# A layer of spectral mixing and two expert layers on one core: y's blocks turned by VectorE and carried by the regrouping DMAs

## The chip, the cores and the metric

One core of a Trainium2 chip runs the whole program. The metric is the time of one execution in microseconds, as the median of several; the profile is of one more execution. TensorE (PE), VectorE (DVE), ScalarE (ACT) and GpSimd (POOL) compute; SyncE (SP) issues nearly all DMAs, in order, on one queue. Each engine runs its own instructions in order and waits for the others by semaphores.

## The reference

An array x of 8 x 3072 x 256 goes through three layers; the random inputs are float32.

```python
X = np.fft.rfft(x, axis=1)                    # 1: spectral mixing
Yr = Xr @ w_r - Xi @ w_i + b_r;  Yi = Xr @ w_i + Xi @ w_r + b_i
Y = shrink(Yr, 0.01) + 1j * shrink(Yi, 0.01)
y = np.fft.irfft(Y, n=3072, axis=1)           # 24576 tokens of 256
h = y @ w_in                                  # 2: 256 -> 2048
x = (h - np.tanh(h)) @ w_out                  #    2048 -> 256
logits = x @ phi                              # 3: 32 slots
d = softmax(logits, axis=0)                   # over the tokens
slot_in = d.T @ x                             # 32 x 256
slot_out = experts(slot_in)                   # 8 experts, relu
out = softmax(logits, axis=1) @ slot_out
```

The second layer's output is never stored. Since x = y M - g w_out, with g = tanh(h) and M = w_in w_out, the slots' inputs can be had from running sums of d.T @ g (2048 features) and of d.T @ y (256 features), over all tokens.

## The kernel before

The program has a spectral phase, a token phase and an expert phase. The change lies in the token phase, which runs from about 700 to 2130 us in the profiled execution. It goes through 48 chunks (nch) of 512 tokens. Of each chunk it computes the 2048 gates g from y (the matmuls of L771, by a seven-product scheme, evacuated by ScalarE at L782 and added to by VectorE at L789, then tanh at L793), the logits (L892 from g, L900 from the raw y, tile yr), their running softmax over tokens, and two updates: `accum` adds d.T @ g to acc, `accum_y` adds d.T @ y to accy.

For an update TensorE needs tokens on the partitions, but gates and y have features there. Gates are turned in two steps. VectorE turns 32x32 blocks (`turn_g`, L846) into a tile gt: four feature pairs (p = 0 to 3) make the first half, p = 4 to 7 the second, 8 blocks of 32 features each. Then `regroup` (L860) moves each half by 16 DMAs of SyncE, from 32 partitions to 32 partitions, into four tiles gq. gt is one pool tag with two buffers, used in turn by the halves. The update `dg_mm` (L1020, tile pd) reads gq and the exponentials et.

y is turned in another way: `turn_y` (step TY, two calls a chunk) has TensorE transpose four 128x128 blocks of yr (L812) into a bank pd, and ScalarE copies the bank into a tile yq (L813). `dy_mm` (step DY, L828) multiplies it into unused columns of the logits' bank, and stands right ahead of `dg_mm`.

The order of all this is written out by hand in the table PLAN (L29 to L42). `chunk(c)` walks it once a chunk; an entry such as ("TY", -1, 0) calls `turn_y` for chunk c - 1, and one that has been done is skipped. On each engine the instructions stand in the order of these calls. A buffer's next writer waits for its readers. In the row of a chunk SyncE issues, in order: the first half's regrouping of the running chunk ("reg", 0, 0), a small store, the load of the next y, the second half's regrouping of the chunk before ("reg", -1, 1), and the load of the raw y ("loadr", 0). The step ("D", -1) follows ("DY", -1), and both come some way behind ("reg", -1, 1).

The last chunk takes another way: its gates are turned by TensorE (`turn_pe`) and so is its y.

`turn_exp` keeps the running sum of exponentials, ssum, with one scalar_tensor_tensor a chunk (L972).

Of the kernel before, what the change touches and what calls it, by code (L numbers as in the profile page):

```python
# [26 lines left out]


PLAN = (  # L29
# [8 lines left out]
    ("reg", -1, 1), ("W", 0, 3), ("splitt", 1, 0), ("comb", -1), ("P", 0, 3, 7),  # L38
# [3 lines left out]
)  # L42
TOKENS_BESIDE = {-4: 1, -2: 1, 0: 1, 1: 2, 2: 3, 3: 4}
# [590 lines left out]
def token_phase(tc, nch, yd, wh, wl, wp, wy, ident, ew):  # L634
# [9 lines left out]
    with ExitStack() as ctx:  # L644
# [175 lines left out]
        def dy_mm(c):  # L820


            beside = c < nch - 1
            o = dy[c] = lp[c + 1][:, 256:320] if beside else bank()[:, 0:64]
            y = yq.pop(c)
            for k in range(4):
                for a in (3, 2, 1, 0):
                    nc.tensor.matmul(  # L828
                        o[32 * a:32 * a + 32], ex[c][:, k, :], y[:, a, k], start=k == 0 and not beside, stop=k == 3,
                        skip_group_check=True,  # L830
                    )

        def accum_y(c):
# [3 lines left out]
            else:  # L837
                nc.vector.tensor_copy(accy, o)

        def turn_g(c, p):  # L840
            g = gs[c, p]
            if (c, p // 4) not in gt:
                gt[c, p // 4] = gtp.tile([128, 16, 8, 32], F32, tag="gt", name="gt")
            t = gt[c, p // 4]
            for u in range(2):
                nc.vector.transpose(out=t[:, :, 2 * (p % 4) + u, :], in_=g[:, u, :].rearrange("p (c i) -> p c i", i=32))  # L846

# [4 lines left out]
        def regroup(c, h):  # L852

            t = gt.pop((c, h)).rearrange("p (k q) f i -> p q k (f i)", q=4)
            if h == 0:
                gq[c] = [ew.gq_tile([128, 4, 512]) for _ in range(4)]
            for a in range(4):
                o = gq[c][a][:, :, 256 * h:256 * h + 256]
                for q in range(4):
                    nc.sync.dma_start(out=o[32 * q:32 * q + 32], in_=t[32 * a:32 * a + 32, q])  # L860

        def turn_pe(c, p, engines):

            if p // 4 not in gl:
                gl[p // 4] = gtp.tile([128, 4, 4, 256], F32, tag="gt", name="gl")
            o = gl[p // 4].rearrange("p k a (f i) -> p k f a i", i=32)
            for u in range(2):
                t = bank()
                for k in range(4):
                    k = slice(128 * k, 128 * k + 128)  # L870
                    nc.tensor.transpose(t[:, k], gs[c, p][:, u, k], ident)
                src = t.rearrange("p (k a i) -> p k a i", k=4, a=4)
                dst = o[:, :, 2 * (p % 4) + u]
                if engines[u] is nc.scalar:
                    nc.scalar.activation(dst, src, AF.Copy)
                else:
                    engines[u].tensor_copy(dst, src)
# [86 lines left out]
        def turn_exp(c):  # L964
            e, rs, a = le[c][64:128], rss.pop(c), al.get(c)
            et = sp.tile([128, 4, 32], F32, tag="et", name="et", bufs=1)
            for r in range(2):
                nc.vector.transpose(
                    out=et[64 * r:64 * r + 64].rearrange("p k s -> p (k s)"), in_=e[:, 128 * r:128 * r + 128]
                )  # L970
            if c:
                nc.vector.scalar_tensor_tensor(  # L972
                    out=ssum[0:64], in0=ssum[0:64], scalar=a[0:64], in1=rs, op0=ALU.mult, op1=ALU.add
                )
                nc.vector.tensor_copy(a[64:128], a[0:64])
            else:
                nc.vector.tensor_copy(ssum[0:64], rs)
            ex[c] = et
# [31 lines left out]
        def dg_mm(c):  # L1010

            o = dp[c] = ps2.tile([128, 512], F32, tag="d", name="pd")
            if c < nch - 1:
                parts = [(slice(0, 512), gq.pop(c))]
            else:
                parts = [(slice(256 * h, 256 * h + 256), [gl[h][:, :, a] for a in range(4)]) for h in range(2)]
            for f, g in parts:
                for k in range(4):
                    for a in (3, 2, 1, 0):
                        nc.tensor.matmul(  # L1020
                            o[32 * a:32 * a + 32, f], ex[c][:, k, :], g[a][:, k], start=k == 0, stop=k == 3
                        )
            del ex[c]
# [20 lines left out]
        def do(name, k, *args):  # L1044
# [5 lines left out]
            "P": wino, "A": add, "G": gate, "T": turn_g, "L": logit_mm, "D": dg_mm, "acc": accum, "sum": sum_l,  # L1050
            "sum2": sum_l2, "max": soft_max, "exp": soft_exp, "turnexp": turn_exp, "comb": combine,
            "cexp": combine_exp, "cend": combine_end, "loady": load_y, "rawt": raw_t, "splity": split_y,
            "lowy": low_y, "splitt": split_t, "reg": regroup, "loadr": load_raw, "TY": turn_y, "DY": dy_mm,
            "accy": accum_y,
        }

        def chunk(c):

            for name, d, *args in PLAN:
                k = c + d  # L1060
                if name == "S":

                    if c == 1:
                        split_sw(*args)
                elif name == "W":
                    if c == nch - 1:
                        weights(*args)
                elif k > 0 and k < nch or k == 0 and name not in "PAG":
                    if k < nch - 1 or name not in ("T", "reg"):
                        if c < nch - 1 or name not in ("D", "DY", "accy"):  # L1070
                            do(name, k, *args)
                    if c == 1 and (name, k, *args) == ("L", 0, 4):
                        do("L", 0, 6)
# [121 lines left out]
class ExpertWeights:  # L1195
# [61 lines left out]

    def load_ct(self, c0, c1):
        n = c1 - c0
        u = self.gtp.tile([128, n, 128], F32, tag="gt", name="ect") if c0 else self.gq_tile([128, n, 128])  # L1260
        for c in range(c0, c1, 16):
            m = min(c + 16, c1)
            self.tc.nc.sync.dma_start(out=u[:, c - c0:m - c0], in_=self.ctd[:, c:m])
        for c in range(c0, c1, 8):
            self.cts[c] = u[:, c - c0:c - c0 + 8]
# [5 lines left out]
    def pieces(self, j, home):  # L1271
        def tile(pool, tag, n=1024, **kw):
            t = pool.tile([128, n], F32, tag=tag, name="ewt", **kw)
            return [t[:, 512 * i:512 * i + 512] for i in range(n // 512)]

        if home in self.spare:
            return self.spare.pop(home)
        if home == "t":
            return [u for n in ("th", "tl") for i in range(2) for u in tile(self.txp, f"{n}{i}", 512)]
        if home[0] == "w":  # L1280
            return [u for n in ("wh", "wl") for i in range(2) for u in tile(self.wp, f"{n}{i}{home[1]}", 512)]
        if home == "y":
            return [u for t in ("y", "yh") for u in tile(self.yp, t)]
        if home[0] == "s":
            return tile(self.tyq, home, 1536)
        if home == "gt":
            r = tile(self.gtp, "gt", 4096)
            self.spare["gt"] = r[4:]
            return r[:4]
        if home == "gq":  # L1290
            t = self.gq_tile([128, 2048])
            return [t[:, 512 * i:512 * i + 512] for i in range(4)]
        return [u for i in range(2) for u in tile(self.txp, f"x{(2 * j + i) % 4}")]
# [203 lines left out]
```

## Time and profile before

| | |
|---|---|
| time, median of 3 runs | 2262.81 us (2259.74 to 2264.0) |
| the profiled execution's own time | 2261.4 us |
| its span | 2259.6 us |
| TensorE busy | 2210.0 us (98%) |
| weight loads of TensorE | 1819.3 us (81%) |
| VectorE busy | 1764.8 us (78%) |
| ScalarE busy | 1456.5 us (64%) |
| GpSimd busy | 656.5 us (29%) |
| packets of SyncE's DMA queue | 77.6% of 16 engines' span |

The profile lists each instruction with its engine, line, tiles (out<-in, buffer numbers left out) and shape. The chain that ended last is followed back from the last instruction: it names at each step what released it. PE's and weight loads' busy times overlap. Matmuls are pipelined, so several in a row have starts closer together than one's duration: in a row of TensorE the start of the next row tells what a group took of the engine. [...]

### The profile page before, as it was taken

The page shows a single profiled execution, that of the slowest core. Times are in us where ns is not written, and L with a number is a line of the kernel's source. Part 1 is how long each engine was busy: PE and PEld are TensorE (multiplying, and loading weights), DVE is VectorE, ACT ScalarE, POOL GpSimd, SP SyncE. Part 2 cuts the span into 40 slices and gives each one's busy share as a digit, 9 for nine tenths or more (in the row PEclk, how much of TensorE's full clock was granted, in tenths as well). Part 3 has the DMA queues.
Part 4 walks back from the last instruction along what each step waited for, and adds up shares of the span by engine and source line. Part 5 has one row for each costly group of instructions (what it writes and reads, how often), then busy time and mean ns, then how long its engine had stood idle before and what let it go on. Part 6 is the DMA issues. An engine that isn't in the chain of part 4 may idle for free.

```text
span 2259.6 us, 51262 instructions
## 1 busy us (share of the span) xinstructions
PE 2210.0 (98%) x19832; PEld 1819.3 (81%) x19832; DVE 1764.8 (78%) x3557; ACT 1456.5 (64%) x2395; POOL 656.5 (29%) x666
## 2 busy tenths in 40 slices
PE   6999999999999999999999999999999999999989
PEld 3678888887888888888888888888888888888747
DVE  3999988988995787787777877877778778777634
ACT  2456666666556677777766777676767676767524
POOL 1334333443443322222222222222222222222111
PEclk8999999999999999999999999999999999999999
DMA  8778899898657777777777777778777777777899
GB/s 227 233 226 264 250 267 277 245 261 269 201 186 211 179 168 178 179 181 181 184 172 176 175 178 179 178 180 189 171 177 177 175 179 177 182 186 173 243 341 366
DMA packets 404019, 471.17 MB, mean 209 GB/s; under 512 B 36160, under 2 KB 351808, under 8 KB 403392
## 3 DMA queue, kind: packets, MB, share of 16 engines
q1 hardware_dynamic: 403664, 467.85, 77.6%
q8 instruction: 157, 2.57, 0.5%
q14 instruction: 86, 0.70, 0.1%
q10 hardware_dynamic: 112, 0.04, 0.0%
HBM read 164.45 MB, written 106.17 MB: 120 GB/s over the span
## 4 chain that ended last, share of the span: by engine, by line
PE 87%; DVE 5%; DMA 4%; issue 2%; SPq 1%; ACT 0%; POOL 0%; DVEq 0%; POOLq 0%; ACTq 0%
PE ph L771 41%; PE pl L892 8%; PE pd L1020 8%; PE pmix L322 5%; PE pi L407 4%; PE pf L248 4%; PE pf L281 3%; PE p_out L1319 3%; PE pi L379 3%; PE pa L322 2%; PE pd L812 2%; DMA ewt<-in_moe_w 1%; PE pl L828 1%; DVE sw L372 1%; PE pl L900 1%
## 5 line engine op out<-in xcount | busy, mean ns | idle before, releaser
L782 ACT ACTIVATE g<-ph 128x512 f32<-128x512 f32 x752 | 448.0, 596 | 379.5 <-PE ph L771 354.5
L789 DVE TENSOR_TENSOR g<-ph,g 128x512 f32<-128x512 f32 x564 | 373.3, 676 | 157.7 <-PE ph L771 147.2
L846 DVE STREAM_TRANSPOSE gt<-g 128x512 f32<-128x512 f32 x752 | 476.2, 681 | 13.0 <-DMA gq<-gt 6.5
L771 PE MATMUL ph<-th,s 128*128 128x256 f32 x2256 | 482.0, 286 | 2.1 <-ACT g L782 2.1
L771 PEld LDWEIGHTS ph<-th,s 128*128 128x128 f32 x2256 | 377.8, 189 | 41.4 <-issue 19.4
L793 ACT ACTIVATE g<-g 128x1024 f32<-128x1024 f32 x376 | 392.2, 1053 | 1.5
L771 PE MATMUL ph<-tl,s 128*128 128x256 f32 x1128 | 318.3, 282 | 0.0
L771 PE MATMUL ph<-y,wh 128*128 128x256 f32 x1128 | 316.4, 280 | 0.0
L771 PE MATMUL ph<-yh,wl 128*128 128x256 f32 x1128 | 315.7, 280 | 0.0
L771 PE MATMUL ph<-yh,wh 128*128 128x256 f32 x1128 | 315.7, 280 | 0.0
L684 POOL TENSOR_TENSOR tl<-tr,th 128x512 fp32r<-128x512 f32 x94 | 121.8, 1297 | 383.8 <-ACT th L683 350.3
L372 POOL TENSOR_TENSOR sw<-t,c 64x256 f32<-64x256 f32 x192 | 169.5, 883 | 170.1 <-DVE c L364 131.3
L771 PEld LDWEIGHTS ph<-tl,s 128*128 128x128 f32 x1128 | 213.9, 190 | 0.0
L771 PEld LDWEIGHTS ph<-yh,wh 128*128 128x128 f32 x1128 | 212.8, 189 | 0.1
L771 PEld LDWEIGHTS ph<-yh,wl 128*128 128x128 f32 x1128 | 212.4, 188 | 0.0
L771 PEld LDWEIGHTS ph<-y,wh 128*128 128x128 f32 x1128 | 212.3, 188 | 0.1
L678 POOL TENSOR_TENSOR tr<-y 128x256 f32<-128x256 f32 x92 | 67.8, 737 | 470.3 <-DMA y<-yd 470.3
L892 PE MATMUL pl<-g,wp 128*32 128x256 f32 x3072 | 195.4, 383 | 0.0
L1020 PE MATMUL pd<-gq,et 128*32 128x512 f32 x1504 | 183.8, 598 | 2.1 <-DMA gq<-gt 2.1
L669 POOL TENSOR_TENSOR y<-y,yh 128x1024 fp32r<-128x1024 f32 x46 | 110.6, 2403 | 182.9 <-issue 182.8
L407 PEld LDWEIGHTS pi<-i,v 96*128 96x128 f32 x1024 | 127.5, 191 | 26.0 <-issue 20.8
L281 PEld LDWEIGHTS pf<-f,a 128*128 128x128 f32 x768 | 102.5, 195 | 54.3 <-issue 40.9
(225 smaller groups left out, 4586.0 us busy)
## 6 DMA issues: line engine op xcount, KB each, us to landing
gq<-gt SPq DMA_DIRECT2D x1504, 128.0 KB, 2.5
xt<-in_x SPq DMA_DIRECT2D x64, 384.0 KB, 5.4
vd<-vs SPq DMA_DIRECT2D x96, 256.0 KB, 3.3
v<-vd SPq DMA_DIRECT2D x64, 384.0 KB, 5.4
yd<-yt SPq DMA_DIRECT2D x48, 512.0 KB, 5.6
y<-yd SPq DMA_DIRECT2D x48, 512.0 KB, 4.9
yr<-yd SPq DMA_DIRECT2D x48, 512.0 KB, 3.7
a<-ad SPq DMA_DIRECT2D x47, 512.0 KB, 6.0
```

Of the source, the lines that this page charges most:

```text
L281: nc.tensor.matmul(p[:, :, h, gg, :], t[:, gg, 128 * h:128 * h + 128], f2[:, 128 * g:128 * g + 128], start=True, stop=True,)
L322: nc.tensor.matmul(o, st[u], w[m], start=first and k == 0, stop=last and k == 2)
L372: eng.tensor_tensor(out=v[64 * ri:64 * ri + 64, gg], in0=t[q, e], in1=c[q, e], op=ALU.subtract)
L407: nc.tensor.matmul(p[:, a, :], t[:, 4 * u + a, :], i2[:, 96 * n2:96 * n2 + 128], start=True, stop=True)
L684: nc.gpsimd.tensor_tensor(out=lo, in0=t, in1=hi.bitcast(F32), op=ALU.subtract)
L771: nc.tensor.matmul(o[:, 256 * j:256 * j + 256], a[u][:, 128 * j:128 * j + 128], y[v], start=new and j == 0 and k == 0, stop=n in (2, 3, 4) ...
L782: nc.scalar.activation(e[n], o.rearrange("p (j n) -> p j n", j=2), AF.Copy)
L789: nc.vector.tensor_tensor(out=h, in0=o, in1=h, op=ALU.add)
L793: nc.scalar.activation(g, g, AF.Tanh)
L846: nc.vector.transpose(out=t[:, :, 2 * (p % 4) + u, :], in_=g[:, u, :].rearrange("p (c i) -> p c i", i=32))
L892: nc.tensor.matmul(lp[c][q:q + 32, 0:256], wp[:, 2 * p + f, :], half_of(gs[c, p + f // 2][:, f % 2], h), start=p == 0 and f < 2, stop=Fals ...
L1020: nc.tensor.matmul(o[32 * a:32 * a + 32, f], ex[c][:, k, :], g[a][:, k], start=k == 0, stop=k == 3)
```

## The change

1. y of chunks 0 to 46 is turned by VectorE: `turn_yr` (step TD) turns the two halves of yr, 128x512 each, into two more blocks of the second half's gt tile, which so holds ten blocks of 32 features. The steps TY leave PLAN, and TD stands behind ("A", 0, 3, 2); the other TD entry is done by then.
2. gt gets two tags with a buffer each, gt0 (8 blocks) and gt1 (10).
3. The second half's regrouping DMAs carry 320 columns instead of 256, and the gq tiles have 576 columns a row. `dy_mm` reads the last 64, `dg_mm` the first 512.
4. ssum's update is a tensor_scalar with two scalars per partition.
[...]

```diff
-    ("P", 0, 2, 1), ("L", -1, 6), ("TY", -1, 0), ("sum", -1), ...
+    ("P", 0, 2, 1), ("L", -1, 6), ("sum", -1), ...
-    ("splitt", 1, 1), ..., ("G", 0, 7), ("A", 0, 3, 2), ("P", 0, 3, 3), ("A", 0, 3, 3),
+    ("splitt", 1, 1), ..., ("G", 0, 7), ("A", 0, 3, 2), ("TD", 0), ("P", 0, 3, 3), ("A", 0, 3, 3),
...
-            y = yq.pop(c)
+            if beside:
+                y = [g[:, :, 512:576] for g in gq[c]]
+            else:
+                y = [yq[c][:, a] for a in range(4)]
...
-                        o[32 * a:32 * a + 32], ex[c][:, k, :], y[:, a, k], start=k == 0 and not beside, stop=k == 3,
+                        o[32 * a:32 * a + 32], ex[c][:, k, :], y[a][:, k], start=k == 0 and not beside, stop=k == 3,
...
+        def gt_tile(c, h):
+            if (c, h) not in gt:
+                gt[c, h] = gtp.tile([128, 16, 8 + 2 * h, 32], F32, tag=f"gt{h}", name="gt", bufs=1)
+            return gt[c, h]
+
+        def turn_yr(c):
+
+            t = gt_tile(c, 1)
+            for kk in range(2):
+                nc.vector.transpose(out=t[:, :, 8 + kk, :], in_=yr[c][:, kk].rearrange("p (c i) -> p c i", i=32))
...
-                gq[c] = [ew.gq_tile([128, 4, 512]) for _ in range(4)]
+                gq[c] = [ew.gq_tile([128, 4, 576]) for _ in range(4)]
             for a in range(4):
-                o = gq[c][a][:, :, 256 * h:256 * h + 256]
+                o = gq[c][a][:, :, 256 * h:256 * h + 256 + 64 * h]
...
-                nc.vector.scalar_tensor_tensor(
-                    out=ssum[0:64], in0=ssum[0:64], scalar=a[0:64], in1=rs, op0=ALU.mult, op1=ALU.add
+                nc.vector.tensor_scalar(
+                    out=ssum[0:64], in0=ssum[0:64], scalar1=a[0:64], scalar2=rs, op0=ALU.mult, op1=ALU.add
...
-    nc = bacc.Bacc("TRN2", target_bir_lowering=False, num_devices=1)
+    nc = bacc.Bacc("TRN2", target_bir_lowering=False, num_devices=1, dynamic_dma_scratch_size=1024)
```

TensorE at the first of a chunk's two groups of transposes, between the logits from y (L900, after the change L912) and the next products; before and after:

```order
L892 MATMUL pl<-g,wp 32x256 x8
L900 MATMUL pl<-yr,wy 32x256 x4
L812 MATMUL pd<-ident,yr 128x128 x4
L771 MATMUL ph<-th,wh 128x256
L771 MATMUL ph<-tl,wh 128x256
```

```order
L904 MATMUL pl<-g,wp 32x256 x8
L912 MATMUL pl<-yr,wy 32x256 x4
L771 MATMUL ph<-th,wh 128x256
L771 MATMUL ph<-tl,wh 128x256
L771 MATMUL ph<-th,wl 128x256
```

The four transposes are gone, and the products follow the logits at once; the second group, which stands between two groups of L771 and L892, goes in the same way.

TensorE at the two updates (DY at L828, after the change L831, and D at L1020, L1032), where the regrouped tiles are read; before and after:

```order
L771 MATMUL ph<-yh,wh 128x256
L771 MATMUL ph<-y,wh 128x256
L771 MATMUL ph<-yh,wl 128x256
L828 MATMUL pl<-yq,et 32x64 x16
L1020 MATMUL pd<-gq,et 32x512 x16
```

```order
L771 MATMUL ph<-yh,wh 128x256
L771 MATMUL ph<-y,wh 128x256
L771 MATMUL ph<-yh,wl 128x256
L831 MATMUL pl<-gq,et 32x64 x16
L1032 MATMUL pd<-gq,et 32x512 x16
```

The order is the same, but the y update now reads gq too, so the wait for the regrouping DMAs stands before it and no longer between the two.

VectorE behind the y update's addition (L836, after the change L839), at the end of a chunk's row of PLAN; before and after:

```order
L836 SCALAR_TENSOR_TENSOR accy<-accy,al,pl 128x64
L846 STREAM_TRANSPOSE gt<-g 128x16x32 x2
L789 TENSOR_TENSOR g<-ph,g 128x2x256 x2
L1000 TENSOR_REDUCE cz<-lt 128x4
L1001 TENSOR_SCALAR cz<-cz 128x4
```

```order
L839 SCALAR_TENSOR_TENSOR accy<-accy,al,pl 128x64
L858 STREAM_TRANSPOSE gt<-g 128x16x32 x2
L789 TENSOR_TENSOR g<-ph,g 128x2x256
L852 STREAM_TRANSPOSE gt<-yr 128x16x32 x2
L789 TENSOR_TENSOR g<-ph,g 128x2x256
L1012 TENSOR_REDUCE cz<-lt 128x4
```

The two turns of y stand between the two additions.

## Rows read from the trace of the kernel before

**Rows 1.** The page: busy times by engine, and the last chain by engine.

```profile
PE 2210.0 (98%) x19832; PEld 1819.3 (81%) x19832; DVE 1764.8 (78%) x3557; ACT 1456.5 (64%) x2395; POOL 656.5 (29%) x666
...
PE 87%; DVE 5%; DMA 4%; issue 2%; SPq 1%; ACT 0%; POOL 0%; DVEq 0%; POOLq 0%; ACTq 0%
```

**Rows 2.** Groups, whole run: line, engine, names, shapes, count | busy us, mean ns | idle before.

```profile
L771 PE MATMUL ph<-th,s 128*128 128x256 f32 x2256 | 482.0, 286 | 2.1 <-ACT g L782 2.1
...
L1020 PE MATMUL pd<-gq,et 128*32 128x512 f32 x1504 | 183.8, 598 | 2.1 <-DMA gq<-gt 2.1
...
L812 PE MATMUL pd<-ident,yr 128*128 128x128 f32 x376 | 58.9, 279 | 0.0
```

**Rows 3.** Timeline of TensorE, first transposes of a chunk: start us, duration us, instruction.

```profile
1028.64 0.28 PE L771 MATMUL ph<-yh,wl 128*128 128x256 f32 x1
1028.85 1.07 PE L892 MATMUL pl<-g,wp 128*32 128x256 f32 x16
1029.74 0.61 PE L900 MATMUL pl<-yr,wy 128*32 128x256 f32 x8
1030.29 0.66 PE L812 MATMUL pd<-ident,yr 128*128 128x128 f32 x4
1030.70 0.36 PE L771 MATMUL ph<-th,wh 128*128 128x256 f32 x1
```

**Rows 4.** Timeline of TensorE, second transposes of a chunk.

```profile
1006.27 0.28 PE L771 MATMUL ph<-th,s 128*128 128x256 f32 x1
1006.39 0.60 PE L812 MATMUL pd<-ident,yr 128*128 128x128 f32 x4
1006.92 1.07 PE L892 MATMUL pl<-g,wp 128*32 128x256 f32 x16
1007.92 0.39 PE L771 MATMUL ph<-th,s 128*128 128x256 f32 x1
```

**Rows 5.** Timeline of TensorE, the two updates in two chunks that follow each other.

```profile
1012.38 0.65 PE L828 MATMUL pl<-yq,et 128*32 128x64 f32 x32
...
1042.46 0.65 PE L828 MATMUL pl<-yq,et 128*32 128x64 f32 x32
1042.94 3.87 PE L1020 MATMUL pd<-gq,et 128*32 128x512 f32 x32
```

**Rows 6.** Timeline of SyncE's queue: start us, duration of the issuing us, DMAs.

```profile
1026.24 0.38 SPq L658 DMA_DIRECT2D y<-yd  x1
1026.71 11.13 SPq L860 DMA_DIRECT2D gq<-gt  x16
1037.93 0.53 SPq L800 DMA_DIRECT2D yr<-yd  x1
```

**Rows 7.** Tile gq, 1026.7 to 1037.9 us: from issue to landing.

```profile
DMA to landing us min/median/max: 2.5/3.6/4.3
```

**Rows 8.** Stretches: length, busy time of each engine (x instructions), clock, DMA share, GB/s.

```profile
1028.00:1034.00 6.00, 6.00 (x64) 5.11 (x64) 3.99 (x11) 4.99 (x9) 2.86 (x4) 1.00 1.06 255
1049.00:1054.00 5.00, 5.00 (x59) 3.94 (x59) 4.03 (x10) 3.63 (x6) 1.24 (x1) 1.00 0.87 201
```

**Rows 9.** Timeline of VectorE at the end of a chunk's row.

```profile
1015.09 1.30 DVE L846 STREAM_TRANSPOSE gt<-g 128x512 f32<-128x512 f32 x2
1016.31 0.65 DVE L789 TENSOR_TENSOR g<-ph,g 128x512 f32<-128x512 f32 x1
1019.08 0.69 DVE L789 TENSOR_TENSOR g<-ph,g 128x512 f32<-128x512 f32 x1 [2.12 <-PE ph L771]
```

**Rows 10.** The running sum's update, whole run: count, duration ns min/median/max.

```profile
L972 DVE SCALAR_TENSOR_TENSOR ssum<-ssum,al,rs x47: 210/994/994, 768.2 to 2147.8; 64x1 f32<-64x1 f32 x47
```

**Rows 11.** The last chunk: SyncE's and TensorE's timelines, and a stretch as above.

```profile
2110.77 15.79 SPq L860 DMA_DIRECT2D gq<-gt  x16
...
2129.87 5.65 PE L1020 MATMUL pd<-gq,et 128*32 128x512 f32 x32 [2.08 <-DMA gq<-gt]
...
2110.00:2120.00 10.00, 10.00 (x98) 8.94 (x96) 5.97 (x13) 8.12 (x15) 0.00 (x0) 1.00 1.03 264
```

More of the change, by code (lines that the diff above doesn't have):

```diff
@@ L838, in accum_y @@
                 nc.vector.tensor_copy(accy, o)
+        def gt_tile(c, h):
[6 more added lines that the diff above has]
+                nc.vector.transpose(out=t[:, :, 8 + kk, :], in_=yr[c][:, kk].rearrange("p (c i) -> p c i", i=32))
         def turn_g(c, p):
             g = gs[c, p]
-            if (c, p // 4) not in gt:
-                gt[c, p // 4] = gtp.tile([128, 16, 8, 32], F32, tag="gt", name="gt")
-            t = gt[c, p // 4]
+            t = gt_tile(c, p // 4)
             for u in range(2):
@@ L864, in turn_pe @@
             if p // 4 not in gl:
-                gl[p // 4] = gtp.tile([128, 4, 4, 256], F32, tag="gt", name="gl")
+                gl[p // 4] = gtp.tile([128, 4, 4, 256], F32, tag=f"gt{p // 4}", name="gl", bufs=1)
             o = gl[p // 4].rearrange("p k a (f i) -> p k f a i", i=32)
@@ L1013, in dg_mm @@
             if c < nch - 1:
-                parts = [(slice(0, 512), gq.pop(c))]
+                parts = [(slice(0, 512), [g[:, :, 0:512] for g in gq.pop(c)])]
             else:
@@ L1052, in token_phase @@
             "cexp": combine_exp, "cend": combine_end, "loady": load_y, "rawt": raw_t, "splity": split_y,
-            "lowy": low_y, "splitt": split_t, "reg": regroup, "loadr": load_raw, "TY": turn_y, "DY": dy_mm,
+            "lowy": low_y, "splitt": split_t, "reg": regroup, "loadr": load_raw, "TY": turn_y, "TD": turn_yr, "DY": dy_mm,
             "accy": accum_y,
@@ L1068, in chunk @@
                 elif k > 0 and k < nch or k == 0 and name not in "PAG":
-                    if k < nch - 1 or name not in ("T", "reg"):
+                    if k < nch - 1 or name not in ("T", "TD", "reg"):
                         if c < nch - 1 or name not in ("D", "DY", "accy"):
@@ L1259, in load_ct @@
         n = c1 - c0
-        u = self.gtp.tile([128, n, 128], F32, tag="gt", name="ect") if c0 else self.gq_tile([128, n, 128])
+        u = self.gtp.tile([128, n, 128], F32, tag="gt1", name="ect", bufs=1) if c0 else self.gq_tile([128, n, 128])
         for c in range(c0, c1, 16):
@@ L1286, in pieces @@
         if home == "gt":
-            r = tile(self.gtp, "gt", 4096)
+            r = tile(self.gtp, "gt0", 4096, bufs=1)
             self.spare["gt"] = r[4:]
```

8 rows, old and new, of the table PLAN are left out of this document.

## The prediction

> **What bounds the kernel now.** I read the page first. TensorE is busy 98% of the span, and 87% of the chain that ended last is its work [rows 1]. The reader should see that only time on TensorE's own queue, or a new wait of it, can move the end; VectorE (78%) and ScalarE (64%) are not at the end. Next, the groups of instructions: the eight transposes of a chunk (L812) come 376 times, that is for 47 chunks, and the only wait of TensorE for the regrouped gates in the whole run is 2.1 us at L1020 [rows 2]. Third, one chunk in order of time. The chunk's update L828 starts at 1012.38 and the next at 1042.46: 30.08 us a chunk [rows 5]. Last, SyncE's queue, since the change puts more bytes on it and makes L828 wait for them [rows 6].
>
> **TensorE loses the transposes.** First group: L900 starts at 1029.74, L812 follows 0.55 later and holds the engine until L771 at 1030.70 [rows 3]. After a run of 16 narrow matmuls (L892) L771 starts 1.00 later [rows 4]; 16 of them take 0.89 from the first L892 to L900 [rows 3], so the step from narrow to wide costs 0.11 and eight L900 take 0.445. Without L812, L771 would start 0.445 + 0.11 = 0.56 after 1029.74, at 1030.30 instead of 1030.70: 0.40 saved. Second group: L771, L812, L892 start at 1006.27, 1006.39 and 1006.92, 0.65 from the last L771 to L892 [rows 4]; where no transposes lie between, the same step takes 1028.64 to 1028.85, 0.21 [rows 3]: 0.44 saved. Together 0.84 a chunk. The last chunk keeps its transposes, and those of chunk 46 lie in the period where TensorE waits for DMAs anyway, so 46 x 0.84 = **38.6 us**. The first L771 behind the transposes took 0.36 where its neighbours take 0.28 [rows 3]; if it is held by its bank, and is held longer when it comes sooner, I bound the loss by that 0.08, doubled, a chunk: 31 to 38.6. I take 38.6, because TensorE's idle time at L771 is 2.1 us in the whole run [rows 2].
>
> **VectorE gains two transposes** of 128x512 a chunk. Two such ones (L846) took 1.30 us. They stand right before the add that follows the add at 1016.31; that next add starts only at 1019.08, after 2.12 us of waiting for TensorE's ph [rows 9]. So 1.30 of the 2.12 is filled and 0.8 remains: nothing on the path. Without that cover it would be 1.30 a chunk on a queue that is idle a fifth of the time. The new wait there is for yr's landing. Its DMA is issued at 1037.93, behind the sixteen regrouping DMAs [rows 6], some 9 us ahead of the same place one chunk on (1016.31 + 30.08 = 1046.4); nothing is late. Behind the waiting instruction stand the adds that free ph banks, so a miss would reach TensorE.
>
> **The running sum** took 994 ns in the median and 210 at least for one element a partition [rows 10]. As a tensor_scalar I bound it by these two. Either way it is off the path: it only moves the end of the first half's turning, and so the first DMA of the next regrouping, by up to 0.8 us earlier; that group then waits for TensorE's L1020 to release gq as before. Worth 0. ScalarE loses two copies a chunk, also 0. [...]
>
> **The transfers, and the new wait.** The second half's 16 DMAs go from 128 to 160 KB. L828 now reads gq, so it needs the last of them; before, only L1020 did, 0.48 later [rows 5]. The distances: the last of the 16 is issued near 1037.24 (first at 1026.71, 16 in 11.13 us, a pace of 0.695, the last taking 0.6) [rows 6]; L828 starts at 1042.46, 5.2 us behind it. With TensorE 0.84 sooner there remain **4.4 us**. A regrouping DMA in this stretch lands 2.5 us after its issue at least and 4.3 at most [rows 7]: the load of y, issued just ahead, builds 1.8 us of backlog, which is worked off until the last ones land in 2.5. How fast it is worked off depends on the engines' time per DMA, which no row gives for 160 KB. Regrouping alone runs at 201 GB/s, 0.652 us for 128 KB, at a busy share of 0.87 [rows 8]: 0.567 of work each. Against the pace of 0.695 that works off 16 x 0.128 = 2.0 us, which agrees with the 2.5 at the end. For 160 KB the lower bound is the same 0.567 (if packets cost by number); by bytes it is 1.25 times that, 0.709; at the 255 GB/s that the engines reach while y is in the queue [rows 8] it is 0.643. I take 0.67, between the last two. Then 16 x 0.025 = 0.4 is worked off, the last DMA lands 2.5 + 1.8 - 0.4 = 3.9 us after its issue, and 0.5 of the 4.4 is left. At 0.709 it lands after 4.5: a wait of 0.1. Not every chunk is as regular as this one, so I charge 0.1 a chunk, 46 x 0.1 = **5 us**; bounds 0 and, see below, far more.
>
> [...]
>
> **The tail.** In the last chunk the 16 DMAs lie behind weight loads, and TensorE already waits 2.08 us for them before L1020 [rows 11]. 16 x 32 KB = 0.52 MB more at 264 GB/s [rows 11] is 2.0 us, and L828 (0.48) now comes behind the wait: **2.5 us** lost; bounds 0 and 3. What follows is a queue of weight loads, which shifts with it.
>
> **Sum** for the profiled execution, which took 2261.4 us (span 2259.6): 2261.4 - 38.6 + 5 + 2.5 = 2230.3. The median of the runs shown is 1.4 above it: **2232 us**.
>
> **Rivals.** (A) The second half becomes a transfer bound. [...] For it: a busy share over 1 while y is in the queue [rows 8]. Against: at 255 GB/s the engines do more than the issue asks. Chance 0.19. (B) Slower: the same wait at L828, with the whole pace growing with the bytes, 0.695 x 1.25 = 0.87. The last lands after 4.3 + 16 x 0.175 = 7.1, L828 waits 2.7, and 46 x (2.7 - 0.84) = 86 us are lost besides the tail: 2351. It decides from 0.754 us a DMA on, where the wait (4.3 + 16 x 0.059 - 4.4) equals the 0.84 saved; at 0.77 the wait is 1.1 and the time 2277. Against: the issue instruction, not the transfer, sets the pace now. Chance 0.10. (C) The change does not do what it says for TensorE: the time without transposes turns into waits for ph banks or adds, half of it kept, 2261 + 1.4 - 19 + 5 + 2.5 = 2251. For it: the 0.36 of the first L771 behind the transposes [rows 3]. Against: the 2.1 us of idle time at L771 [rows 2]. Chance 0.07.
>
> **How the numbers follow.** The forecast has 0.64. It spans 2224 (no wait, tail free: 2262.8 - 38.6) to 2241. Range 2223 to 2256: with the forecast it takes in about two thirds of (A) and most of (C), and leaves out (B) and (A)'s end. About 0.2%, 4.5 us, is what a measurement of this kernel can tell from no change. Faster: 0.64 + 0.13 + 0.06 = 0.83; within: 0.07; slower: 0.10.
>
> **What would show it.** A chunk period near 29.3 us; L900 followed by L771 within 0.57, and L771 by L892 within 0.21; no idle time of VectorE before the turn of yr; the 16 DMAs issued in about 11 us, the last landing under 4.4 us; idle time of TensorE before the update that reads gq under 10 us in total. It is wrong if that idle time is 20 us or more (A, B), or if the idle time before L771 grows (C).

## The result: slower by 0.9%, where 1.4% faster was forecast

The changed kernel takes 2281.86 us, median of ten runs (2273.93 to 2303.08), against 2261.69 before (2259.07 to 2266.32): a ratio of 1.0093, 95% interval 1.0066 to 1.0119. The profiled execution took 2282.07 us, its span is 2280.3 against 2259.6. The forecast was 2232 with a range of 2223 to 2256.

The page of the changed kernel, busy times and the last chain by engine, to be held against [rows 1]:

```profile
PE 2179.1 (96%) x19456; PEld 1770.7 (78%) x19456; DVE 1791.3 (79%) x3651; ACT 1414.9 (62%) x2301; POOL 656.5 (29%) x666
...
PE 40%; SPq 9%; DVE 9%; DMA 7%; ACT 2%; issue 1%; ACTq 0%; DVEq 0%
```

TensorE has 31 us less to do, and yet its share of the last chain fell from 87% to 40%, while SyncE's queue rose to 9% and VectorE to 9%. TensorE is no longer the only bound. Its waits for the y update (line, releaser: us in total, times, longest):

```profile
PE pl L831 <- DMA gq<-gt: 32.2, 19, 4.0
PE pl L831 <- DVE g L789: 9.5, 10, 2.4
PE pl L831 <- DVE lt L998: 8.4, 8, 1.2
PE pl L831 <- DVE cm L1002: 1.4, 1, 1.4
```

The update L831 waits 51.5 us in 38 of 47 chunks; before, TensorE waited 2.1 us for regrouped tiles in the whole run [rows 2]. The rows that name VectorE are the same wait: the instructions named there (the addition, the turning for the softmax over slots) had ended and give L831 nothing, and in 32 of the 38 chunks the last landing lies within 0.3 us of L831's start (in the other six the last DMA's landing has no record, and the last one recorded lies within 1.0).

Two pieces of TensorE's timeline show that the transposes went as forecast (start us, duration us, instruction):

```profile
1588.79 0.28 PE L771 MATMUL ph<-th,s 128*128 128x256 f32 x1
1589.00 1.93 PE L904 MATMUL pl<-g,wp 128*32 128x256 f32 x32
...
1598.33 0.61 PE L912 MATMUL pl<-yr,wy 128*32 128x256 f32 x8
1598.88 0.38 PE L771 MATMUL ph<-th,wh 128*128 128x256 f32 x1
```

L904 follows L771 by 0.21 (0.65 with transposes between [rows 4]), L771 follows L912 by 0.55 (0.96 with them, 1029.74 to 1030.70 in [rows 3]). So the gain is there: 0.44 + 0.41 a chunk. Some chunks earlier, SyncE's queue, and the y update in TensorE's timeline:

```profile
1522.13 12.93 SPq L872 DMA_DIRECT2D gq<-gt  x16
1535.18 0.53 SPq L1018 DMA_DIRECT2D ctd<-le  x1
1535.82 0.37 SPq L658 DMA_DIRECT2D y<-yd  x1
1536.28 12.66 SPq L872 DMA_DIRECT2D gq<-gt  x16
```

```profile
1551.99 0.82 PE L831 MATMUL pl<-gq,et 128*32 128x64 f32 x29 [0.79 <-DMA gq<-gt]
```

The second half's sixteen DMAs take 12.66 us to issue, where they took 11.13 [rows 6], and L831 waits 0.79 us although the last issue ended 3.05 us before.

**The round that closes.** The first half's fifth DMA needs a gq tile that D of the chunk before frees: there are five tiles, and each chunk takes four. SyncE waits for that in every chunk, before and after the change (SyncE's waits; first of the kernel before, then of the changed one):

```profile
SPq L860 <- PE pd L1020: 55.9, 46, 1.6
```

```profile
SPq L872 <- PE pd L1032: 133.9, 46, 7.5
```

So there is a closed round: D's end, the rest of the first half's DMAs, the small store and y's load, the second half's DMAs, their landing, DY, D. A lateness at its end comes back at its beginning. Its parts, means over 45 chunks from the records of the traces, in us (the period is the time from one DY's start to the next; where the last landing has no record, in six chunks of the changed kernel, the last one recorded stands for it):

| | before | changed | 128 KB (below) |
|---|---|---|---|
| DY's start to D's end | 4.36 | 4.52 | 4.09 |
| D's end to the fifth DMA | 0.04 | 0.04 | 0.06 |
| to the first half's last issue | 8.20 | 8.22 | 8.20 |
| to the second half's first | 1.38 | 1.37 | 1.37 |
| the second half's issue | 11.32 | 12.56 | 11.48 |
| last issue to last landing | 2.23 | 3.53 | 2.08 |
| landing to DY's start | 2.56 | 0.29 | 1.73 |
| period of a chunk | 30.08 | 30.53 | 29.01 |

Before, the round was 27.5 us long and had 2.56 to spare under TensorE's 30.08. After, its two DMA terms grow by 1.24 and 1.30, and the round, but for 0.29, is the period: nothing of TensorE's gain is left, and what disturbs a landing is no longer absorbed.

The round closes a second way too, through the engines' own order. The second half can't be issued before VectorE has turned the last of its blocks, and by the records that turn ends 9.25 to 9.27 us behind D's end in every one of these chunks, in all three kernels. By way of gq the second half starts 9.6 us behind D's end, only 0.4 later.

### The profile page after: what moved, and what is told of

Its sections match the earlier page's. It is cut to its first block, busy times and chain, and to the rows that moved or that the text cites. A ratio compares the mean times of both kernels' runs of the same rounds, so it can differ in the third digit from the quotient of the medians.

```text
span 2280.3 us, 50462 instructions
## 1 busy us (share of the span) xinstructions
PE 2179.1 (96%) x19456; PEld 1770.7 (78%) x19456; DVE 1791.3 (79%) x3651; ACT 1414.9 (62%) x2301; POOL 656.5 (29%) x666
## 4 chain that ended last, share of the span: by engine, by line
PE 40%; SPq 9%; DVE 9%; DMA 7%; ACT 2%; issue 1%; ACTq 0%; DVEq 0%
PE ph L771 23%; SPq L872 9%; PE pd L1032 7%; DVE gt L858 5%; PE pl L904 4%; DMA gq<-gt 4%; PE p_out L1331 3%; DVE g L789 2%; PE pl L831 2%; DMA ewt<-in_moe_w 1%; ACT g L782 1%; DMA yr<-yd 1%; PE pl L912 1%; DVE et L980 1%; ACT g L793 0%
## 5 line engine op out<-in xcount | busy, mean ns | idle before, releaser
L858 DVE STREAM_TRANSPOSE gt<-g 128x512 f32<-128x512 f32 x752 | 476.3, 681 | 14.5 <-DMA gq<-gt 7.2
L771 PE MATMUL ph<-th,s 128*128 128x256 f32 x2256 | 481.7, 286 | 1.7 <-ACT g L782 1.6
L771 PEld LDWEIGHTS ph<-th,s 128*128 128x128 f32 x2256 | 377.9, 189 | 41.0 <-ACT g L793 19.3
L771 PE MATMUL ph<-tl,s 128*128 128x256 f32 x1128 | 318.4, 282 | 0.0
L771 PE MATMUL ph<-y,wh 128*128 128x256 f32 x1128 | 316.3, 280 | 0.0
L771 PE MATMUL ph<-yh,wh 128*128 128x256 f32 x1128 | 315.8, 280 | 0.5 <-DVE g L789 0.5
L771 PE MATMUL ph<-yh,wl 128*128 128x256 f32 x1128 | 315.8, 280 | 0.0
L771 PEld LDWEIGHTS ph<-tl,s 128*128 128x128 f32 x1128 | 213.6, 189 | 0.0
L771 PEld LDWEIGHTS ph<-yh,wh 128*128 128x128 f32 x1128 | 212.9, 189 | 0.8 <-DVE g L789 0.8
L771 PEld LDWEIGHTS ph<-yh,wl 128*128 128x128 f32 x1128 | 212.5, 188 | 0.0
L771 PEld LDWEIGHTS ph<-y,wh 128*128 128x128 f32 x1128 | 212.3, 188 | 0.1
L904 PE MATMUL pl<-g,wp 128*32 128x256 f32 x3072 | 195.4, 383 | 0.0
L1032 PE MATMUL pd<-gq,et 128*32 128x512 f32 x1504 | 184.6, 623 | 0.0
```

Source lines behind the costliest of these rows:

```text
L771: nc.tensor.matmul(o[:, 256 * j:256 * j + 256], a[u][:, 128 * j:128 * j + 128], y[v], start=new and j == 0 and k == 0, stop=n in (2, 3, 4) ...
L904: nc.tensor.matmul(lp[c][q:q + 32, 0:256], wp[:, 2 * p + f, :], half_of(gs[c, p + f // 2][:, f % 2], h), start=p == 0 and f < 2, stop=Fals ...
L1032: nc.tensor.matmul(o[32 * a:32 * a + 32, f], ex[c][:, k, :], g[a][:, k], start=k == 0, stop=k == 3)
```

## The experiments

The theory was that bytes on this round make the loss. The rivals: the place of DY (it needs the landing 0.5 us sooner than D did, and TensorE is sooner); the transfers as such, round or no round; VectorE's two transposes; the small parts.

**128 KB again.** What is changed:

```diff
...
-            t = gt.pop((c, h)).rearrange("p (k q) f i -> p q k (f i)", q=4)
+            t = gt.pop((c, h))[:, :, 2 * h:].rearrange("p (k q) f i -> p q k f i", q=4)
...
-                o = gq[c][a][:, :, 256 * h:256 * h + 256 + 64 * h]
+                o = gq[c][a][:, :, 256 * h:256 * h + 256].rearrange("p k (f i) -> p k f i", i=32)
```

> The changed kernel, with the second half's DMAs carrying 128 KB again: ten blocks are turned, but two blocks of gates are left out of the transfer and y's two take their place, so part of the update is computed from the wrong blocks. DY still reads gq and still needs the last DMA; VectorE still turns y; TensorE's transposes are gone. Theory (bytes on a closed loop: D's end frees gq, the next first half's DMAs, y's load, the second half's DMAs, their landing, DY, D; 27.5 us round before, 30.2 after): the round is back at 27.5 to 28, below TensorE's 29.2, no waits at DY beyond some 5 us, 2224 to 2232 us. Rival 1 (it is the place, not the bytes: DY needs the landing 0.5 us sooner than D did and TensorE is 0.84 sooner, so the ordinary spread of landings hits it): over 2250 us, idle time at DY over 20 us. Rival 2 (VectorE's two more transposes): 2275 to 2285 us.

Measured: 2213.49 us, ratio 0.9789 (0.9771 to 0.9807). TensorE's and SyncE's timelines of one chunk:

```profile
1033.07 0.65 PE L831 MATMUL pl<-gq,et 128*32 128x64 f32 x32
1033.54 3.62 PE L1032 MATMUL pd<-gq,et 128*32 128x512 f32 x32
...
1062.07 0.65 PE L831 MATMUL pl<-gq,et 128*32 128x64 f32 x32
```

```profile
1046.45 11.20 SPq L872 DMA_DIRECT2D gq<-gt  x16
```

The chunk takes 29.00 us, and L831 waits 0.8 us in the whole run. The place of DY and VectorE's transposes cost nothing: 68 us lie in the 32 KB. The time is even below the theory's 2224, since D is shorter too, 3.62 us against 3.87 [rows 5] (see the last section).

**The bytes without the rest.** TensorE's transposes are put back and DY reads them; the 160 KB travel, and nobody reads y out of them.

```diff
...
-            if beside:
-                y = [g[:, :, 512:576] for g in gq[c]]
-            else:
-                y = [yq[c][:, a] for a in range(4)]
+            y = [yq[c][:, a] for a in range(4)]
```

> The changed kernel, with TensorE's transposes of y put back and DY reading them; VectorE still turns y and the DMAs still carry it in 160 KB, but nobody reads it. D alone needs the landing. Theory (bytes on the loop): issue of the second half 12.4 to 12.7 us and landing 3 us behind, the round without DY 29.6 us against TensorE's 30.07: only the disturbed chunks wait, now at D, 5 to 15 us in all: 2265 to 2280 us. Rival 1 (place, not bytes): 2260 to 2264 us, no waits at D.

Measured: 2278.74, ratio 1.0076 (1.0061 to 1.0091); the period is 30.37, issue 12.67 and landing 3.50, near the changed kernel's. D now waits, as the theory said:

```profile
PE pd L1029 <- DMA gq<-gt: 9.4, 11, 1.9
```

So 17 us are lost by the bytes in a kernel whose TensorE has as much to do as before (VectorE still turns y here, but the run before shows that this costs nothing).

**gq's release taken off the round.** gq becomes two tiles a chunk: the first half's with two buffers, so that its DMAs need not wait for D of the chunk before, and the second half's with one. D is done in 32 matmuls of 256 columns.

```diff
...
-                gq[c] = [ew.gq_tile([128, 4, 576]) for _ in range(4)]
+            gq[c, h] = ew.half_tile(c, h)
...
+        return self.gqp.tile([128, 4, 4, 256 + 64 * h], F32, tag="qb" if h else f"qa{c % 2}", name="gq")
...
```

> The changed kernel, with gq kept as two tiles per chunk: the first half's in two buffers, the second half's (with y) in one; D in 32 matmuls of 256 columns in place of 16 of 512; DMA scratch 512 B. The first half's DMAs then need not wait for D's end of the chunk before; bytes and DMAs are the same. Theory (loop): the loop is cut, the second half is issued up to 2 us sooner, waits at DY shrink to under 15 us, 2222 to 2240 us. Rival 2 (the transfers as such are the bound, engines' time for 160 KB): waits stay, 2270 to 2290 us.

**The same, and D's first half ahead of the wait.** As before, and in PLAN:

```diff
-    ("DY", -1), ("D", -1), ("accy", -1)
+    ("D", -1, 0), ("DY", -1), ("D", -1, 1), ("accy", -1)
```

> As the kernel with gq in two tiles, and D's first half, which reads only the first half's DMAs, put ahead of DY: 1.8 us of TensorE's work stand before the wait. Theory (loop): waits at DY vanish but for a few us, 2220 to 2232 us, below the kernel before. Rival 2 (transfers as such): the wait is covered by 1.8 us but the pace stays the transfers', 2255 to 2285 us.

Measured: 2243.14 (ratio 0.9919, 0.9896 to 0.9941), and 2216.64 (0.9802, 0.9788 to 0.9817) with D's first half ahead. TensorE's waits for the second half, first in the one (two rows of five, which make 14.5 us in 18 chunks together), then in the other kernel:

```profile
PE pl L831 <- DMA gq<-gt: 8.7, 8, 2.9
PE pl L831 <- DVE g L789: 1.9, 3, 0.9
```

```profile
PE pl L831 <- DMA gq<-gt: 1.0, 3, 0.5
```

A chunk of the latter on TensorE:

```profile
1529.19 1.93 PE L1033 MATMUL pd<-gq,et 128*32 128x256 f32 x32
1530.94 0.63 PE L831 MATMUL pl<-gq,et 128*32 128x64 f32 x32
1531.39 1.91 PE L1033 MATMUL pd<-gq,et 128*32 128x256 f32 x32
```

The mean period is 29.45 in the first and 29.07 in the second, though issue (12.4 and 12.5 us) and packets are nearly as in the changed kernel. The transfers as such are therefore no bound.

The theory's range for the first was 3 us too low (its profiled execution lay inside, with a span of 2234.6), and the step that it rested on did not come: the second half is not issued up to 2 us sooner. D, VectorE's turning and SyncE's queue in that kernel:

```profile
1508.72 3.66 PE L1031 MATMUL pd<-gq,et 128*32 128x256 f32 x63
...
1520.34 1.29 DVE L858 STREAM_TRANSPOSE gt<-g 128x512 f32<-128x512 f32 x2
...
1506.57 11.51 SPq L871 DMA_DIRECT2D gq<-gt  x16
...
1521.66 11.94 SPq L871 DMA_DIRECT2D gq<-gt  x16
```

The first half no longer waits for D's end, which is at 1512.38. But VectorE's last turn ends at 1521.63, 9.25 us behind D's end as ever, and the second half starts with it; so it is, within 0.05 us, in 39 of 44 chunks. The edit took one way of closing off the round and left the other, and the second half starts only 0.3 us sooner behind D's end, 9.3 in place of 9.6. The split gives back 1.08 of the 1.53 us a chunk between 30.53 and 29.00: 0.3 by this earlier start, some 0.7 in issue and landing together and 0.3 in DY and D, of which 0.2 are lost again between landing and DY. The first half and y's load are issued 1.2 us earlier, which may be why the landings come sooner; that was not tested.

In the second kernel 1.75 us of TensorE's work stand ahead of the wait, and D's end lies 2.4 us behind DY's start in place of 4.5. That shortens the round itself, to 27.4 us in a period of 29.07, and gives back most of the rest. This kernel beats the one before by 2.0% and the changed one by 2.9%.

**Is it the split alone?** The same two edits in the kernel before, with y turned by TensorE:

> The kernel before, y turned by TensorE as ever, with gq in two tiles a chunk, D in two halves and its first half ahead of DY, DMA scratch 512 B. It has no wait for the regrouping to hide. Theory: TensorE-bound, D's waits a little cheaper: 2246 to 2264 us. Rival (the split of gq itself, not the turn of y by VectorE, gives the 2217 of the kernel with both): under 2235 us.

Measured: 2261.50, ratio 1.0002 (0.9993 to 1.0011). The split gives nothing where nothing waits; it only lets the turn of y by VectorE pay.

**The small parts.** The changed kernel with the old update of the running sum, and the kernel before with only the new update and the scratch (`dynamic_dma_scratch_size=1024`):

> The changed kernel, with the running sum's update left a scalar_tensor_tensor, as before the change. Theory (bytes on the loop): the update takes 1.0 us again in the median in place of 0.27, but stands ahead of the first half's turning, and the first half's DMAs beyond the fourth wait for D's end, not for that turning; 2275 to 2290 us, no difference to the changed kernel's 2282 beyond its spread. Rival (the small parts matter: a shorter VectorE queue moves the regrouping ahead): at least 5 us apart from 2282.

> The kernel before, with only the two small parts of the change: the tensor_scalar and the DMA scratch of 1 KB. Theory: TensorE-bound with 2.5 us between landing and DY, nothing moves: 2258 to 2265 us. Rival (they carry part of the result): over 0.2% either way.

Measured: 2279.08 (ratio 1.0087, 1.0052 to 1.0122) and 2261.84 (1.0002, 0.9992 to 1.0013). Neither part shows in the result. The update's duration in the changed kernel, and VectorE's turn of y, whole run (count, ns min/median/max; busy us, mean ns, idle before):

```profile
L984 DVE TENSOR_SCALAR ssum<-ssum,al,rs x47: 266/269/269, 767.3 to 2168.9; 64x1 f32<-64x1 f32 x47
...
L852 DVE STREAM_TRANSPOSE gt<-yr 128x512 f32<-128x512 f32 x94 | 60.3, 680 | 0.2 <-DMA yr<-yd 0.2
```

**y's load on another queue.** It stands on the round, between the halves; here ScalarE's queue issues it.

```diff
-            nc.sync.dma_start(out=t.bitcast(F32), in_=yd[c // 6][c % 6])
+            (nc.scalar if c > 1 else nc.sync).dma_start(out=t.bitcast(F32), in_=yd[c // 6][c % 6])
```

> The changed kernel, with the load of the next y issued by ScalarE's queue and not by SyncE's, where it stands on the loop between the two halves (0.4 us of issue, 1.2 to 1.5 us from the first half's last issue to the second half's first, with the small store). Theory (loop): the round shrinks by 0.4 to 0.5 us at least, 46 x 0.45 = 20 us sooner, 2250 to 2270 us; the second half also waits for VectorE's turning, which may take some of it. Rival (the transfers' total in these stretches is the bound, whatever the queue): no gain, 2275 to 2295 us, landings later by what the issue gains.

Measured: 2299.37, ratio 1.0170 (1.0133 to 1.0206), outside the theory's range and past the rival's. SyncE has a new wait:

```profile
SPq L872 <- DMA y<-yd: 88.9, 46, 3.8
```

In each chunk one of the first half's DMAs waits some 1.9 us for y's landing, and the first half takes 10.1 us from the fifth DMA on instead of 8.2; the gap between the halves, the issue and the landing behind it are 0.5, 0.5 and 0.6 shorter. The sum is a round of some 30.5 us, period 30.69. These DMAs don't touch y's tile. The records show what they wait for: in all 41 chunks where y's landing is on record, the DMA that waits is the one that signals its own landing on the semaphore of y's load, and it starts 0.02 us behind that landing. The round is again what sets the period, but the experiment made it longer in another place and says little of the load's own price.

**Half of the added bytes.** Nine blocks of the ten, 144 KB: once the last nine, once the first nine.

```diff
...
-            t = gt.pop((c, h)).rearrange("p (k q) f i -> p q k (f i)", q=4)
+            t = gt.pop((c, h))[:, :, h:].rearrange("p (k q) f i -> p q k f i", q=4)
...
-                o = gq[c][a][:, :, 256 * h:256 * h + 256 + 64 * h]
+                o = gq[c][a][:, :, 256 * h:256 * h + 256 + 32 * h].rearrange("p k (f i) -> p k f i", i=32)
```

> The changed kernel, with the second half's DMAs carrying 144 KB (nine of the ten blocks: one block of gates is left out of the transfer, so part of the update is computed from wrong blocks). Theory (bytes on the loop): the round lies half way between that of 128 KB (27.3 us) and that of 160 KB (30.2 us), 28.7, under TensorE's 29.0 by 0.3; regular chunks don't wait, disturbed ones do: 2220 to 2245 us, and most of the 68 us between 128 and 160 KB falls between 144 and 160 KB. Rival (the cost is proportional to the bytes, no bound that is crossed): half way, 2240 to 2255 us.

> As the kernel with 144 KB, but the nine blocks that are carried are the first nine of ten and not the last nine, so a row is read from its start and not 128 B behind it (y's second block is the one left out, DY computes from one wrong block). Bytes, DMAs and waits are the same. Theory A (with 1152 B a row the cost is in the length): packets stay at 83 to 90 ns, 2250 to 2268 us, as with the last nine. Theory B (the start of a row at an odd 128 B costs): packets of 78 to 82 ns and a round under TensorE's 29.0 us, 2220 to 2245 us.

Measured: 2260.58 (ratio 0.9991, 0.9973 to 1.0008) and 2260.56 (0.9995, 0.9983 to 1.0008). Both the theory's half way and the rival's missed: the cost isn't linear in the bytes. (The profiled executions, 2269 and 2268 us, were the slowest of the ten of each, so their traces show somewhat more than the medians lost.) Issue and landing together, means over 46 chunks, are 13.55 us at 128 KB, 15.86 at 144 and 16.09 at 160. Where the row starts doesn't matter, the second run shows. The packets' own times are 73, 85 and 95 ns for 1024, 1152 and 1280 B, so about by bytes; with 128 packets a DMA on 16 engines that is 0.59, 0.68 and 0.76 us. At 128 KB, and at 160 in the kernel with TensorE's transposes, landings follow each other by 0.59 and 0.76 us, as the packets have it; at 144 KB by 0.735, not 0.68. What those landings wait for beyond their packets stays open.

**Another order of the sixteen DMAs**, so that neighbours in the queue lie in different 32 partitions, in the changed kernel (second half, shown here) and in the one with D's first half ahead (both halves):

```diff
-            for a in range(4):
...
-                for q in range(4):
+            for i in range(4):
+                for j in range(4):
+                    a, q = (j, (i + j) % 4) if h else (i, j)
...
```

> The changed kernel, with the second half's sixteen DMAs in another order: neighbours in the queue read from different 32 partitions and write to different 32 partitions (before, four in a row read the same 32). Bytes, number and waits stay. [...] Theory B (the time goes by bytes in the engines, wherever they lie): packets stay at 88 to 95 ns, 2272 to 2292 us.

> The kernel with gq in two tiles and D's first half ahead of DY, with both halves' DMAs in that spread order. [...] Theory B: 2213 to 2220 us, the same.

Measured: 2289.36 (ratio 1.0110, 1.0093 to 1.0126) and 2216.89 (0.9796, 0.9781 to 0.9811). Packets stay at 95 ns in the first, and in the second at the 93 that they take without the new order. In the first the sixteen take 11.6 us to issue and the last lands 4.9 us behind, together 16.4, no less than the changed kernel's 16.1. So the packets are not longer for the reason that four DMAs in a row read the same 32 partitions. Whether it matters that one DMA's packets all lie in the same 32 was not tested.

## Why the prediction was wrong, step by step

**What bounds the kernel**: right for before. The rows held the round too, since SyncE's wait for D's end 46 times was in the same list of waits; I used D's release of gq in one sentence on the running sum and never added up the round that it closes.

**TensorE loses the transposes**: right, 0.41 and 0.44 a chunk where 0.40 and 0.44 were worked out, and no loss by banks. The gain was forecast 0.24 too small, because D got shorter as well: 29.00 us a chunk is the floor, not 29.24.

**VectorE, the running sum, the scratch**: right, all at nothing: the update and the scratch alone gave 2261.84 us, a ratio of 1.0002. The update took 269 ns, near the lower of its two bounds; the turn of y waited 0.2 us in the whole run.

**The transfers, and the new wait**: the step that failed. I charged 0.1 us a chunk for the wait; measured, the period stands 1.53 us above TensorE's 29.00. Three terms were wrong. First, the time of a 160 KB DMA: I took 0.67 us, between 0.643 and 0.709. The upper value, by bytes from the row of 201 GB/s, was near; the lower was read from a stretch of 255 GB/s, in which y's load moved 4096 B in 159 ns a packet beside the regrouping's 1024 in 71 (medians of the packets' records). Its rate says nothing of short rows. Stretches of regrouping alone, before and after (packets, MB, share of 16 engines, over 7.00 us each):

```profile
q1 hardware_dynamic: 1528, 1.39, 88.8%
```

```profile
q1 hardware_dynamic: 1288, 1.46, 94.3%
```

These are 0.888 x 7.00 / 1.39 = 4.47 us a MB and 0.943 x 7.00 / 1.46 = 4.52: the same by bytes, so 0.59 us for 128 KB and 0.74 for 160. Second, the pace of the issue: I held it at 0.695 us, and it became 12.56 / 16 = 0.785. What slows it is open: at 144 KB and in the spread order the sixteen took only 11.6 us, with the last landing 4.3 and 4.9 us behind them, so it is not just how far the landings lag. From the first issue to the last landing I had 15 x 0.695 + 3.9 = 14.3 us; it took 16.1. Third, the distance of 4.4 us was measured along one chunk, as if the second half started at its old time; on a closed round a wait is handed on to the next chunk, by gq's release as by TensorE's and VectorE's own order.

**A term that was missing**: TensorE's granted clock, a share of full speed. It was 1.00 over the whole token phase of the kernel before (700 to 2130 us). In the changed one D ran slower behind some long waits (length, busy times with counts, clock, DMA share, GB/s; behind a wait of 3.27 us, and behind one of 1.53):

```profile
1613.50:1620.40 6.90, 6.85 (x73) 3.95 (x74) 3.37 (x6) 0.06 (x1) 0.00 (x0) 0.75 0.52 86
...
1645.80:1651.00 5.20, 5.09 (x71) 2.90 (x72) 4.20 (x8) 0.39 (x1) 0.00 (x0) 1.00 0.47 102
```

The 0.75 is a mean: the granted clock was 0.50 from 1613.54 on for 3.41 us, and 1.00 behind that. In 7 of 47 chunks DY and D take 5.8 to 6.1 us at a mean clock of 0.71 to 0.72, in place of 4.1 to 4.4 at 1.00; that is about 12 us in all, and D lies on the round. All seven stand behind waits of 2.1 us or more; behind two others, of 2.3 and 3.2 us, the clock was 1.00.

**The tail**: 2.5 us forecast. The last period grew from 31.78 to 35.87, 4.1, of which 3.0 came back behind it: 1.1.

**The sum.** Against the forecast's 2230.3 the profiled execution is 52 us longer: 45 x (1.53 - 0.1) = 64 for the round, -11 for the shorter D, -2 for tail and start: 51.

**The rivals.** (B), chance 0.10, came nearest: a wait at the y update, with the pace of the DMAs growing with the bytes. Its rule, a wait that outweighs the gain from 0.754 us a DMA on, met the packets' 0.76; at 0.77 it gave 2277. But it too measured the distance along one chunk and has no round in it, and its own price of 2351 was 69 us too high, so that 2277 lies near the measured time is in part luck. (A), chance 0.19, had the same wait with the pace of the issue as before: an estimate of 0.75 us a DMA, 1.25 times the 0.60 of one issue, gave a wait of 0.8 in every chunk and 2264. The packets' 0.76 met its time of a DMA, but it lacked the slower issue and the round. (C) didn't happen.

## What to carry to other kernels

When a change puts bytes on a queue, add up the closed round that the queue stands in (the work that frees the buffers, the issues, the landing, the work that waits) and compare it with the period: its slack, here 2.56 us, and not the distance in one chunk, is what the change may use. Look for every way in which the round closes: freeing the buffers started the transfers only 0.3 us sooner here, because the engines' own order closes it almost as tightly. Price short-row DMAs by stretches with the same rows alone, since a mixed stretch borrows its rate from the longer ones (here 255 GB/s with y's load in it, 201 without). And a wait that can't be removed is cheap if independent work of the same engine can be moved ahead of it and so off the round: with gq split, 1.75 us of D ahead of the wait made the same change worth 2.0% instead of costing 0.9%.

## What the hardware showed beside

D is shorter when DY carries the wait for the sixteen DMAs. In the kernel before, the matmuls of D's four column groups start 0.00, 0.23, 0.27 and 0.27 us behind the first (each reads another gq tile) and keep this to the end: the next L771 starts 4.28 us behind DY. With 128 KB, where DY reads gq first and doesn't wait, the groups of D start within 0.02 and L771 comes 4.02 behind; in the changed kernel's chunks that wait, within 0.11 and 4.24 (where the granted clock is 1.00). D's second half in the kernel before with split gq took 2.15 us, in the changed one 1.91. That the groups' separate waits make the stagger fits these runs, but was not tested alone.
